# Zero matmuls from a bank of their own up to batch 0's KV products, w_phi's 64-row copy loaded first, and a new order of all steps

## The chip, the cores and the metric

The kernel runs on one core of a Trainium2 chip. The metric is the device time of one execution in microseconds (us); lower is better. Five engines work side by side, each with its own queue of instructions that it takes in order: TensorE (PE, matmuls, with its weight loads shown as PEld), VectorE (DVE), ScalarE (ACT), GpSimd (POOL) and SyncE (SP, which here only issues DMAs; POOL and ACT issue some too). Matmul results go to PSUM, which has eight banks.

## The reference

Attention with a feature map for 8 batches of 8 heads, 576 tokens and 64 channels, and behind it a gated feed-forward layer (FFN) over all 4608 tokens.

```
def phi(x):
    proj = einsum('bhsd,df->bhsf', x, w_phi)            # 64 -> 128 features
    proj = proj - max(abs(proj), axis=-1)
    return concat([exp(proj), exp(-proj)])
q_p, k_p = phi(q), phi(k)
kv  = einsum('bhsf,bhsd->bhfd', k_p, v)
num = einsum('bhsf,bhfd->bhsd', q_p, kv)
den = einsum('bhsf,bhf->bhs', q_p, sum(k_p, axis=2)) + 1e-06
x   = (num / den) as [4608, 512]
out = (max(x @ w_gate, 0) * (x @ w_val)) @ w_out        # 512 -> 1536 -> 512
```

## The kernel before

The whole kernel is one list of some two thousand steps, written out in a string `ORDER`. A loop at its end reads the words one after the other and calls the function of that name, so that the order of the words is the order of the instructions in each engine's queue. A word such as `ke.0.1.2.0:3@kp0` means the step `ke` with the arguments 0, 1, 2, 0, in PSUM bank 3, taking slot 0 of the ring of buffers `kp`. The semaphore waits follow from the data. A step waits for the data that it reads, and for the readers of the bank or buffer that it overwrites. Behind a waiting step everything of the same engine waits too.

The steps that this text speaks of, by engine, with their lines in the profile. The first argument is the batch b. The second, for k, is the group j of heads: group 0 has heads 0 and 1 and the 64 last tokens of all heads, group 1 heads 2 to 4, group 2 heads 5 to 7.

- Loads by POOL, which also turn fp32 into bf16: `lk` (heads of k, into `kn`), `lm` (last tokens of k), `lq` (q), `lv.0` (v of batch 0), `wl.0.i` and `wl.1.i` (thirds of w_val and w_gate), `wo` (thirds of w_out).
- Loads by SP: `wp` (w_phi in 32-row copies, into `w32f`, L373), `wq` (w_phi in two 64-row copies, into `w64f`, L379), `lw` (last tokens of v, into `vm`), `lv.b` for later batches (a quarter of v each), `gt` (a tiny DMA that reads `kn`, so that SP goes on only when these heads of k are there), `od` (output).
- PE: `zz.n` (n matmuls of 256 columns of zeros into a bank, whose result nobody reads, L408), `k0` (transposes of batch 0's k, L533), `k2` (k times w_phi for group j, with `w64`, into four banks, L554), `kr` (the same for later batches), `qs` and `qc` (w_phi times q, L694, with `w32`), `qy` (transposes the maxima), `kv` (the KV products of a group, L658), `nu` (numerators and denominators, L757), `xp` (transposes of x, L822), `pv` and `pg` (FFN for 128 tokens, L945), `fv`, `fg` and `fo` (FFN for 512 tokens, L916 and L977), `fp` (half of the output's columns, L1006).
- ACT: `ke` (exponentials of a k bank, 384 columns, into `kp`, L563), `qe` (of a q bank, 512 columns, into `qp`, L709), `kk` and `kp` (exponentials of k's maxima), `kc` (KV from PSUM, L669), `qw`, `xa`, `va`, `pa`, `oc` (copies out of PSUM), `kw` (L541, the same copy as `k1`; no word of the order before uses it).
- DVE: `wd` and `wc` (casts of `w64f` and `w32f`, L385 and L382), `if` (identity in fp32), `k1` (transposed k from PSUM to `kT`, 768 columns, L536), `kx` (maxima of a k bank, L571), `qt` and `kt` (transposes), `qx` (maxima of a q bank, L717), `vd`, `vp` (v times the exponentials, for group 2), `nt`, `nv`, `nr` (numerators and denominators put together), `vb`, `pc`, `xc`, `kd`, `oe` (copies out of PSUM; each does the same as an ACT step: `va`, `pa`, `xa`, `kc`, `oc`), `ga` and `pb` (gate times value).
- POOL's arithmetic: `id` (identity), `vs`, `vo`, `vr` (v times the exponentials of k's maxima; the KV products read these), `nx` (x, L800).

In batch 0's front, k comes in by groups; each is transposed on PE (`k0`), copied to SBUF (`k1`) and multiplied with w_phi (`k2`); ACT and DVE read the four banks (`ke`, `kx`); q follows through `qs`, `qe` and `qx`; then come the KV products, the numerators, the transposes of x and the first pieces of the FFN. In between there are five groups of zero matmuls in the order before: 37 in bank 0, then 5, 6, 7 and 7 in banks 1, 4, 5 and 1. Later batches' attention is interleaved with the FFN of the batches ahead.

## Time and profile before

| what | value |
| --- | --- |
| time, median of 3 runs | 378.46 us (378.4 to 378.5) |
| the profiled execution | 378.79 us, its span 376.8 us |
| PE busy | 367.3 us, 97% of the span |
| DVE, ACT, POOL busy | 296.3, 222.6 and 161.4 us |
| mean granted clock of TensorE | 0.986 |
| chain that ended last | PE 89%, DVE 5%, ACT 4%, DMA 2% |

The span runs from the first to the last instruction, and the rest of the time lies around it. Durations below are those of the profiled execution. A profile line with a source line such as L563 belongs to the step named with that line above.

### The profile page before, as it was taken

The page shows a single profiled execution, that of the slowest core. Times are in us where ns is not written, and L with a number is a line of the kernel's source. Part 1 is how long each engine was busy: PE and PEld are TensorE (multiplying, and loading weights), DVE is VectorE, ACT ScalarE, POOL GpSimd, SP SyncE. Part 2 cuts the span into 40 slices and gives each one's busy share as a digit, 9 for nine tenths or more (in the row PEclk, how much of TensorE's full clock was granted, in tenths as well). Part 3 has the DMA queues.
Part 4 walks back from the last instruction along what each step waited for, and adds up shares of the span by engine and source line. Part 5 has one row for each costly group of instructions (what it writes and reads, how often), then busy time and mean ns, then how long its engine had stood idle before and what let it go on. Part 6 is the DMA issues. An engine that isn't in the chain of part 4 may idle for free.

```text
span 376.8 us, 9181 instructions
## 1 busy us (share of the span) xinstructions
PE 367.3 (97%) x3591; PEld 197.2 (52%) x3591; DVE 296.3 (79%) x680; ACT 222.6 (59%) x539; POOL 161.4 (43%) x180
## 2 busy tenths in 40 slices
PE   8788999999999999999999999999999999999996
PEld 6457857546544645455435554464444644444443
...
PEclk9859999999999999999999999999999999999999
...
DMA packets 90513, 38.04 MB, mean 101 GB/s; under 512 B 64230, under 2 KB 85734, under 8 KB 90470
## 3 DMA queue, kind: packets, MB, share of 16 engines
...
q10 hardware_dynamic: 144, 0.13, 0.1%
...
## 4 chain that ended last, share of the span: by engine, by line
PE 89%; DVE 5%; ACT 4%; DMA 2%; issue 0%; SPq 0%; DVEq 0%; ACTq 0%
PE bank L916 46%; PE bank L977 22%; PE bank L658 6%; PE bank L757 4%; PE bank L945 4%; PE bank L694 3%; ACT kp L563 2%; PE bank L511 2%; DMA w64f<-in_w_phi_dram 2%; DVE mk L571 1%; ACT qp L709 1%; PE bank L1006 1%; PE bank L898 1%; DVE u L788 1%; DVE maxq L717 1%; DVE t L778 1%
## 5 line engine op out<-in xcount | busy, mean ns | idle before, releaser
L563 ACT ACTIVATE kp<-bank 128x384 bf16<-128x384 f32 x192 | 83.2, 513 | 26.2 <-PE bank L511 15.0
L977 PE MATMUL bank<-wo,h 128*128 128x512 bf16 x420 | 98.3, 379 | 0.0
L937 DVE SCALAR_TENSOR_TENSOR h<-bank,val 128x512 bf16<-128x512 f32 x100 | 66.3, 681 | 29.8 <-PE bank L916 25.5
L916 PE MATMUL bank<-xTs,wg 128*128 128x512 bf16 x352 | 86.7, 379 | 0.0
L916 PE MATMUL bank<-xTs,wv 128*128 128x512 bf16 x352 | 86.2, 379 | 0.0
L800 POOL TENSOR_TENSOR xu<-u,r 128x512 bf16<-128x512 f32 x36 | 37.5, 1044 | 97.3 <-DVE r L796 92.4
L931 ACT CAST val<-bank 128x512 bf16<-128x512 f32 x70 | 41.6, 606 | 62.2 <-PE bank L916 50.8
L709 ACT ACTIVATE qp<-bank 128x512 bf16<-128x512 f32 x128 | 70.9, 632 | 10.1 <-DVE maxq L717 5.1
L618 POOL TENSOR_TENSOR vs<-vn,ek 128x780 bf16<-128x780 f32 (+3 forms) x40 | 53.0, 1338 | 37.8 <-ACT ek L580 35.1
L977 PEld LDWEIGHTS <-h 128*128 128x128 bf16 x420 | 39.1, 98 | 44.0 <-issue 0.9
L916 PEld LDWEIGHTS <-wv 128*128 128x128 bf16 x400 | 37.0, 98 | 43.2 <-issue 3.5
L916 PEld LDWEIGHTS <-wg 128*128 128x128 bf16 x400 | 37.4, 98 | 42.0 <-issue 1.8
L571 DVE TENSOR_REDUCE mk<-bank 128x3 f32<-128x384 f32 x96 | 49.0, 539 | 4.3 <-ACT kp L563 2.2
L717 DVE TRANSPOSE_TENSOR_REDUCE maxq<-bank 128x16 f32<-128x512 f32 x64 | 42.3, 692 | 3.5 <-PE bank L694 2.3
L986 ACT COPY ob<-bank 128x512 f32<-128x512 f32 x23 | 13.6, 593 | 37.5 <-PE bank L977 37.2
L788 DVE TENSOR_TENSOR u<-bank,t 128x195 f32<-128x195 f32 (+1 forms) x108 | 33.4, 330 | 1.9
L778 DVE TENSOR_TENSOR t<-bank,cq 128x195 f32<-128x195 f32 (+1 forms) x96 | 29.8, 327 | 5.0 <-PE bank L757 4.1
L757 PEld LDWEIGHTS <-qp 128*128 128x128 bf16 x512 | 24.1, 98 | 13.6 <-issue 2.0
L757 PE MATMUL bank<-kv,qp 128*128 128x65 bf16 x512 | 27.2, 194 | 1.2 <-ACT qp L709 0.8
L934 DVE CAST val<-bank 128x512 bf16<-128x512 f32 x30 | 20.2, 678 | 8.4 <-PE bank L916 8.3
L658 PEld LDWEIGHTS <-kp 128*128 128x128 bf16 x640 | 24.0, 101 | 3.7 <-DVE h L937 0.3
L658 PE MATMUL bank<-vs,kp 128*128 128x65 bf16 x512 | 24.2, 199 | 0.0
...
## 6 DMA issues: line engine op xcount, KB each, us to landing
...
```

The source lines that it names most:

```text
L563: nc.scalar.activation(kp_of(3 * b + j)[:, i, s].rearrange("p n f -> p (n f)"), bank[bk[0]][:, 0 : 3 * F], AF.Exp, scale=(1.0, -1.0)[s],)
L571: nc.vector.tensor_reduce(mk_of(3 * b + j)[:, :, i], bank[bk[0]][:, 0 : 3 * F].rearrange("p (n f) -> p n f", f=F), axis=AX.X, op=ALU.max, ...
L618: nc.gpsimd.tensor_tensor(vs_of(3 * b + j)[:, s, 0:n].rearrange("p n i e -> p (n i) e")[:, :, 0:e], src[:, lo:hi].rearrange("p h i e -> p ...
L658: nc.tensor.matmul(out_ps[:, h - lo, s, :], lhsT=lhsT, rhs=rhs, start=(at == 0), stop=(at == 2 * n * (C + 1) - 1),)
L709: nc.scalar.activation(qp_of(4 * b + i)[:, s, 4 * hq : 4 * hq + 4].rearrange("p h m -> p (h m)"), bank[bk[0]], AF.Exp, scale=(1.0, -1.0)[s],)
L717: nc.vector.tensor_reduce(maxq[:, :, i, 4 * hq : 4 * hq + 4].rearrange("p t h -> p h t"), bank[bk[0]].rearrange("p (h t u) -> p h t u", h= ...
L757: nc.tensor.matmul(bank[bk[0]][:, E * n : E * (n + 1)], lhsT=qp_of(4 * b + i)[:, s, h, :], rhs=kv_of(b)[:, h, s, :],)
L800: eng.tensor_tensor(xu_of(n).rearrange("p (h d) -> p h d", d=D), u_of(n)[:, :, 0:D], r_of(n).to_broadcast([P, H, D]), op=ALU.mult,)
L916: nc.tensor.matmul(bank[bk[0]], lhsT=w[:, dc, P * f : P * f + P], rhs=xT(g)[:, dc, :], start=(dc == 0), stop=(dc == NDC - 1),)
L931: nc.scalar.copy(val_of(NFC * g + f), bank[bk[0]])
L937: nc.vector.scalar_tensor_tensor(h2_of(g, f), bank[bk[0]], 0.0, val_of(NFC * g + f), op0=ALU.max, op1=ALU.mult)
L977: nc.tensor.matmul(bank[bk[0]], lhsT=h2_of(g, f)[:, P * t : P * t + P], rhs=wo_sb[:, f, :], start=(f == 0), stop=(f == NFC - 1),)
```

## The change

Only the string `ORDER` does other work than before; four new functions (`wr`, `lf`, `cf`, `cg`: other ways to load w_phi and the first heads of k) are defined, and no word of the new order names them.

- Zeros: ten groups in place of five, 26, 5, 1, 9, 4, 12, 3, 8, 10 and 5, 83 matmuls instead of 62. The first group is in bank 0, all others are in bank 1. No other step uses bank 1 from the start until `qy.0.2:1`, behind the first two KV products of batch 0 and the first numerators.
- w_phi: `wq` is SP's first DMA. `wp` comes behind `gt.0`, and `wc` behind `qt.0.0` on DVE.
- POOL's loads: `lk.0.0` is the second instead of the fourth, `lk.0.2` stays third, `lm.0.1` fourth, `lq.0.1` fifth instead of second, `lv.0.1` sixth, `lm.0.0` seventh. `lk.1.3`, `wl.1.0` and `wl.0.1` come ahead of all `vs` steps, `wl.0.0` behind them.
- SP's loads: the four quarters of batch 1's v follow each other behind `lw.0.1` and `lw.0.0`; before, two others stood behind `gt.0`, and the last two behind `lw.1.0`, which waits for the `vr` steps.
- The copy of group 0's transposed k goes from DVE (`k1.0`) to ACT (`kw.0`).
- The order of everything else, with its banks and slots, is drawn up anew, down to the last step. 74 copies out of PSUM are done by the other of ACT and DVE: `kw` for `k1`, and `va` and `vb`, `kc` and `kd`, `oc` and `oe`, `xa` and `xc`, `pa` and `pc` for each other. No other step is added or removed.

The diff of the front and of the last steps; the order between is left out:

```diff
--- before
+++ after
 ORDER = """
-ms.0 ms.2 ms.3@vr0 lk.0.1 ms.6 wp wq ms.4@vr1 wd ms.5 lq.0.1 wc id if zz.37:0 k0.1:0 k1.1:0@kT0
-zz.5:1 k2.1:0123 lk.0.2 ke.0.1.1.0:1@kp0 ke.0.1.2.0:2 ke.0.1.3.0:3 ke.0.1.0.0:0 qt.0.1@qT0
-ke.0.1.3.1:3 kx.0.1.1:1@mk0 lk.0.0 kx.0.1.2:2 ke.0.1.2.1:2 ke.0.1.1.1:1 lm.0.1 zz.6:4 k0.2:4
-k1.2:4@kT0 zz.7:5 k2.2:4567 ke.0.2.2.0:6@kp1 kx.0.1.3:3 ke.0.2.3.1:7 lm.0.0 lq.0.0 kx.0.1.0:0
-kx.0.2.0:4@mk1 ke.0.1.0.1:0 lw.0.0 k0.0:2 k1.0:2@kT0 zz.7:1 k2.0:2013 kk.0.1.1@ek0 ke.0.2.1.1:5
-qt.0.0@qT1 kx.0.2.3:7 ke.0.2.2.1:6 kx.0.2.2:6 kx.0.0.0:2@mk2 lv.0.1 ke.0.0.2.1:1@kp2 ke.0.2.1.0:5
-lm.1.0 lv.0.0 ke.0.0.3.1:3 ke.0.0.1.0:0 ke.0.2.0.0:4 lv.0.2 ke.0.0.0.1:2 kk.0.1.0 lm.1.1 wl.1.0
-kx.0.2.1:5 kp.0.2.1:7 ke.0.0.0.0:2 ke.0.2.0.1:4 lw.0.1 qs.0.1.0:6 kx.0.0.1:0 kx.0.0.3:3 qx.0.1.0:6
-vs.0.1.1@vs0 kp.0.2.0:7 qs.0.0.1:5 qe.0.0.1.0:5@qp0 gt.0 lk.1.3 qs.0.0.2:2 lv.1.2 kx.0.0.2:1
-ke.0.2.3.0:7 vp.2:7@vs1 kk.0.0.1@ek1 vs.0.1.0 ke.0.0.2.0:1 qs.0.0.0:4 wl.0.1 kk.0.0.0 ke.0.0.3.0:3
-qx.0.0.0:4 qx.0.0.2:2 vo.0@vs2 vd.0.2.0:7 ke.0.0.1.1:0 qs.0.1.1:1 qe.0.0.1.1:5 qe.0.0.0.1:4@qp1
-qx.0.1.1:1 qs.0.1.2:3 qe.0.1.2.0:3@qp2 qe.0.0.0.0:4 qs.0.0.3:0 qe.0.0.3.0:0@qp3 wl.0.0 qe.0.1.0.0:6
-qs.0.1.3:4 qx.0.0.1:5 qe.0.0.3.1:0 vd.0.2.1:7 qe.0.1.0.1:6 qe.0.1.1.0:1 vr.0.0.0 vr.0.0.1 qy.0.0:5
-qx.0.1.2:3 vr.0.1.0 qx.0.1.3:4 vr.0.1.1 kv.0.2:7 kc.0.2:7@kv0 vo.1 kv.0.1:6 qz.0.0:5@my0 qu.0.0@mz0
-qw.0.0@cq0 qx.0.0.3:0 kt.1.1@kT0 nu.0.0.2:7 nt.0.0.2:7@t0 qe.0.1.3.1:4 qy.0.1:0 qz.0.1:0@my0
-vs.0.0.1 kc.0.1:6 ku.1@kT1 vs.0.0.0 kv.0.0:5 qe.0.1.3.0:4 nu.0.0.1:6 nt.0.0.1:6@t1 kc.0.0:5
-qe.0.0.2.0:2 qu.0.1@mz0 qw.0.1 qy.0.2:0 qe.0.1.1.1:1 nv.0.0.1:6@u0 qe.0.1.2.1:3 qy.0.3:4 nu.0.0.0:5
-nt.0.0.0:5@t2 qe.0.0.2.1:2 nv.0.0.2:7 nv.0.0.0:5 nr.0.0@r0 nu.0.1.1:1 qz.0.2:0@my0 qu.0.2@mz0 lv.1.0
-nt.0.1.1:1@t2 qz.0.3:4@my0 nu.0.1.2:5 qw.0.2 nv.0.1.1:1@u1 lq.1.2 nt.0.1.2:5@t0 kr.1.1:7630
-nx.0.0@xu0 ke.1.1.3.1:0@kp2 wl.1.1 ke.1.1.0.0:7 nu.0.1.0:2 nt.0.1.0:2@t2 nu.0.2.0:4 xp.0.0:1
-xa.0.0:1 nv.0.1.2:5 nv.0.1.0:2 wo.0 nu.0.2.1:5 nr.0.1@r0 nx.0.1@xu0 kx.1.1.3:0@mk2 wl.0.2 nu.0.2.2:2
-lm.2.0 nt.0.2.1:5@t2 ke.1.1.3.0:0 nt.0.2.2:2@t0 nt.0.2.0:4@t1 ke.1.1.1.1:6 lm.2.1 qu.0.3@mz0
-kx.1.1.2:3 pv.1.0:1 pa.1.0:1@val0 ke.1.1.1.0:6 nv.0.2.0:4@u1 nv.0.2.1:5 nv.0.2.2:2 nr.0.2@r0
-pg.0.0:0 nx.0.2@xu1 kx.1.1.0:7 kx.1.1.1:6 qw.0.3 xp.0.1:1 nu.0.3.1:4 xa.0.1:1 ke.1.1.0.1:7
 ...
+ms.0 ms.3@vr0 ms.5 wq ms.6 ms.4@vr1 ms.2 wd lk.0.1 id zz.26:0 k0.1:0 if k1.1:0@kT0 lk.0.0 zz.5:1
+k2.1:0234 ke.0.1.2.0:3@kp0 kx.0.1.3:4@mk0 ke.0.1.0.1:0 lk.0.2 zz.1:1 k0.2:5 kx.0.1.1:2 ke.0.1.2.1:3
+k1.2:5@kT0 ke.0.1.1.0:2 ke.0.1.3.0:4 ke.0.1.1.1:2 kx.0.1.2:3 ke.0.1.3.1:4 lm.0.1 zz.9:1 k2.2:5673
+ke.0.2.1.0:6@kp1 lq.0.1 ke.0.2.2.0:7 ke.0.2.0.0:5 lv.0.1 lm.0.0 kx.0.1.0:0 zz.4:1 k0.0:4
+kk.0.1.1@ek0 ke.0.2.2.1:7 qt.0.1@qT0 kx.0.2.3:3@mk1 kx.0.2.1:6 ke.0.1.0.0:0 gt.0 lq.0.0 kx.0.2.0:5
+kw.0:4@kT0 kx.0.2.2:7 qt.0.0@qT1 kp.0.2.1:3 ke.0.2.1.1:6 zz.12:1 k2.0:4702 wp wc kx.0.0.3:2@mk2
+lv.0.0 kk.0.1.0 kx.0.0.1:7 ke.0.2.0.1:5 ke.0.0.2.1:0@kp2 kx.0.0.2:0 ke.0.0.0.0:4 ke.0.0.3.0:2 lw.0.1
+lv.0.2 lk.1.3 ke.0.2.3.0:3 kp.0.2.0:3 wl.1.0 wl.0.1 vs.0.1.1@vs0 zz.3:1 qs.0.1.0:5 qx.0.1.0:5
+ke.0.0.3.1:2 qs.0.0.0:6 qx.0.0.0:6 kx.0.0.0:4 ke.0.0.2.0:0 qe.0.1.0.0:5@qp0 vs.0.1.0 qe.0.0.0.1:6
+kk.0.0.1@ek1 ke.0.0.1.1:7 qe.0.1.0.1:5 vd.0.2.1:3@vs1 vs.0.0.1@vs2 zz.8:1 qs.0.0.1:2 kk.0.0.0
+vr.0.1.0 vo.1 qs.0.0.2:0 ke.0.0.1.0:7 qx.0.0.1:2 lw.0.0 qx.0.0.2:0 vr.0.0.0 vr.0.1.1 vr.0.0.1 lv.1.2
+ke.0.0.0.1:4 vd.0.2.0:3 qe.0.0.0.0:6 vo.0 qe.0.0.2.1:0@qp1 zz.10:1 qs.0.1.1:5 qx.0.1.1:5
+ke.0.2.3.1:3 qe.0.0.2.0:0 vp.2:3 qs.0.0.3:7 qs.0.1.2:4 qe.0.1.2.1:4 qe.0.1.2.0:4 qe.0.0.1.0:2@qp2
+qs.0.1.3:6 kt.1.1@kT0 zz.5:1 qy.0.0:3 qz.0.0:3@my0 qu.0.0@mz0 kv.0.2:0 qx.0.1.3:6 kv.0.1:3
+qx.0.1.2:4 qx.0.0.3:7 kc.0.2:0@kv0 qw.0.0@cq0 nu.0.0.2:0 qe.0.1.1.0:5 vs.0.0.0 kc.0.1:3 kv.0.0:4
+nt.0.0.2:0@t0 nu.0.2.1:3 kt.1.0@kT1 nv.0.0.2:0@u0 qe.0.0.1.1:2 kc.0.0:4 qy.0.2:1 qz.0.2:1@my0 wl.0.0
+nu.0.0.1:2 qu.0.2@mz0 qe.0.1.1.1:5 qe.0.0.3.1:7@qp3 lq.1.2 nt.0.0.1:2@t0 nu.0.0.0:4 nt.0.0.0:4@t1
+nv.0.0.1:2 nv.0.0.0:4 nr.0.0@r0 qy.0.1:0 lv.1.0 lm.1.1 nu.0.1.1:5 nu.0.1.0:1 qw.0.2 qe.0.1.3.1:6
+qe.0.1.3.0:6 qz.0.1:0@my0 qu.0.1@mz0 qw.0.1 nu.0.1.2:2 qe.0.0.3.0:7 nt.0.2.1:3@t1 qy.0.3:4
+qz.0.3:4@my0 nv.0.2.1:3@u1 nt.0.1.2:2@t0 nt.0.1.0:1@t1 nx.0.0@xu0 xp.0.0:3 xa.0.0:3 nt.0.1.1:5@t2
+nv.0.1.0:1@u0 kr.1.1:7640 ke.1.1.0.0:7@kp2 nv.0.1.1:5 nv.0.1.2:2 nu.0.2.2:1 nt.0.2.2:1@t2 lv.1.3
+ke.1.1.3.0:0 nu.0.2.0:3 lm.1.0 nt.0.2.0:3@t0 nr.0.1@r0 nv.0.2.2:1 wl.1.1 pv.1.0:5 qu.0.3@mz0
+ke.1.1.2.0:4 nv.0.2.0:3 ke.1.1.1.1:6 nx.0.1@xu0 nr.0.2@r1 kx.1.1.1:6@mk2 nu.0.3.1:2 pg.0.0:1 qw.0.3
+nt.0.3.1:2@t0 nx.0.2@xu1 xp.0.1:3 kx.1.1.0:7 pa.1.0:5@val0 wl.0.2 nv.0.3.1:2@u0 ln.0.0 ke.1.1.1.0:6
+xa.0.1:3 ke.1.1.0.1:7 pv.0.0:5 pa.0.0:5@val1 kx.1.1.3:0 ln.0.1 ke.1.1.3.1:0 nu.0.3.0:3 xp.0.2:2
+xa.0.2:2 kx.1.1.2:4 kk.1.1.1@ek1 nt.0.3.0:3@t0 nu.0.3.2:7 ke.1.1.2.1:4 pg.0.1:6 nt.0.3.2:7@t2
+pv.0.1:0 nv.0.3.0:3 wl.1.2 qt.1.1@qT0 pa.0.1:0@val2 pb.0.0:1 qc.1.1:4235 qe.1.1.3.1:5@qp3
+qe.1.1.2.1:3@qp1 nv.0.3.2:7 nr.0.3@r1 qx.1.1.0:4 pb.0.1:6 qe.1.1.3.0:5 ku.1 pv.0.2:1 pv.1.1:7
+pa.0.2:1@val2 kt.1.2@kT0 lv.1.1 qx.1.1.2:3 nx.0.3@xu1 qe.1.1.0.1:4@qp2 pa.1.1:7@val1 qe.1.1.0.0:4
+pg.0.2:6 xp.0.3:1 pb.0.2:6 xa.0.3:1 qe.1.1.2.0:3 pg.1.0:0 qx.1.1.3:5 qt.1.0@qT0 pg.1.1:4
 ...
+va.7.8:0@val3 vb.7.4:4@val1 fo.7.0.0:4 ga.7.4:2@hs12 ga.7.6:7@hs13 fo.7.1.1:1 ga.7.8:3@hs1
+fo.7.1.2:1 fo.7.3.1:6 oe.7.1:1@ob2 od.7.1 fo.7.0.1:4 fp.7.2.1:1 o2.7.2:1@ob1 d2.7.2 fo.7.3.2:6
+fo.7.0.2:4 oc.7.0:4@ob2 od.7.0 oc.7.3:6@ob0 od.7.3 fp.7.2.0:1 o1.7.2:1 d1.7.2
 """
 ...
@@ -378,6 +379,9 @@
     def do_wq(bk):
         nc.sync.dma_start(out=w64f, in_=w_phi[None].to_broadcast([2, D, F]))
+    def do_wr(bk):
+        nc.scalar.dma_start(out=w64f, in_=w_phi[None].to_broadcast([2, D, F]))
+
     def do_wc(bk):
         nc.vector.tensor_copy(w32.rearrange("p a f -> p (a f)"), w32f.rearrange("p a f -> p (a f)"))
@@ -418,6 +422,31 @@
             out=kn_of(b)[:, lo:hi],
             in_=k[b, lo:hi, 0:SF, :].rearrange("h (p c) d -> p h c d", c=C),
         )
+
+    def k_first():
+        flat = xT_mix.rearrange("p a b -> p (a b)").bitcast(FP32)[:, 0 : 3 * C * D]
+        return flat.rearrange("p (h x) -> p h x", h=3)
+
+    def do_lf(bk):
+        lo, hi = HEADS[1]
+        nc.sync.dma_start(
+            out=k_first().rearrange("p h (c d) -> p h c d", d=D),
+            in_=k[0, lo:hi, 0:SF, :].rearrange("h (p c) d -> p h c d", c=C),
+        )
+
+    def cast_first(copy, half):
+        lo, hi = ((0, 2), (2, 3))[half]
+        at = HEADS[1][0]
+        copy(
+            kn_of(0)[:, at + lo : at + hi].rearrange("p h c d -> p h (c d)"),
+            k_first()[:, lo:hi],
+        )
+
+    def do_cf(bk, half):
+        cast_first(nc.vector.tensor_copy, half)
+
+    def do_cg(bk, half):
+        cast_first(nc.scalar.copy, half)
     def do_lq(bk, b, hq):
         lo, hi = (4 * hq, 4 * hq + 4) if hq < 2 else (0, H)
```

More of the change, by code (lines that the diff above doesn't have):

```diff
@@ new lines @@
+fv.3.1:4 kd.4.2:0 qy.4.0:1 qe.4.1.0.0:3 kt.5.1@kT0 lk.6.3 nu.4.3.2:0 qz.4.0:1@my0 qu.4.0@mz0
+fg.3.0:2 qe.4.1.0.1:3 ga.3.0:2@hs5 qw.4.0@cq0 nt.4.3.2:0@t0 nv.4.3.2:0@u2 nu.4.1.0:3 fg.3.1:1
+qe.4.1.1.1:7 nu.4.3.0:2 nt.4.3.0:2@t1 kc.4.1:6 fv.3.7:6 nv.4.3.0:2 va.3.1:4@val3 ga.3.1:1@hs6
+nt.4.1.0:3@t1 qe.4.1.2.1:5 fg.3.7:0 qe.4.1.2.0:5 qe.4.1.1.0:7 nu.4.0.1:1 lv.5.2 lv.5.3 lv.5.0
+va.3.7:6@val0 ga.3.7:0@hs10 nu.4.0.2:7 nu.4.1.1:6 nt.4.1.1:6@t0 nu.4.1.2:5 nt.4.1.2:5@t3
+nv.4.1.1:6@u0 nv.4.1.0:3 fv.3.4:2 fg.3.4:0 va.3.4:2@val0 nt.4.0.1:1@t0 lm.6.0 kr.5.0:2364
```

418 lines of the change are left out of this document (202 added, 216 removed).

## The prediction

> **What bounds the kernel now.** First the page's slices of the span: busy tenths of TensorE (PE), and its granted clock.
>
> ```profile
> PE   8788999999999999999999999999999999999996
> PEclk9859999999999999999999999999999999999999
> ```
>
> PE is full but for the first four slices and the last, and only slices two and three have a lower clock. The busy time by stretches (columns: length, then PE, weight loads, DVE, ACT, POOL, then clock, DMA share, GB/s) puts numbers to it:
>
> ```profile
> 0.00:32.00 32.00, 25.80 (x288) 17.08 (x289) 24.25 (x59) 22.17 (x56) 23.57 (x36) 0.84 1.15 192
> 32.00:377.00 345.00, 341.52 (x3309) 180.14 (x3305) 272.01 (x621) 200.42 (x484) 137.81 (x145) 1.00 0.55 92
> ```
>
> After 32 us PE idles 3.48 us, of which about 3.2 is the tail behind the last matmul (it ends at 373.66 of 376.8). So there PE is the bound, its matmuls are the same in both kernels, and what a new order can win lies ahead of 32 us: it is by how much earlier PE gets enough real work. In that front the chain of waits reads:
>
> ```profile
> 1.56 6.35 DMA w64f<-in_w_phi_dram
> ...
> 9.72 3.95 ACT kp L563 x10
> 13.77 3.06 ACT kp L563 x8
> ...
> 22.09 1.00 PE bank L694 x2
> 23.09 0.40 PE bank L727
> 23.50 3.30 PE bank L658 x60
> ...
> 27.18 0.65 PE bank L658 x20
> ```
>
> First a wait for the 64-row copy of w_phi, then 12 us of ACT's exponentials without a gap, then PE: 60 KV matmuls at 55 ns each, and 20 more at 33 ns. The timeline of ACT shows what that slow PE costs it, and the timeline of DVE the wait at the start (the bracket is the idle time before):
>
> ```profile
> 25.18 0.48 ACT L669 CAST kv<-bank 128x390 bf16<-128x390 f32 x1 [0.71 <-PE bank L658]
> 26.83 0.48 ACT L669 CAST kv<-bank 128x390 bf16<-128x390 f32 x1 [0.57 <-PE bank L658]
> ...
> 7.94 0.23 DVE L385 CAST w<-w64f 128x128 bf16<-128x128 f32 x1 [4.60 <-DMA w64f<-in_w_phi_dram]
> ```
>
> Between 9.72 and 30.3 ACT is idle for 1.28 us in all: these two gaps. Stretches of 3.41 us show how the clock goes with PE's activity:
>
> ```profile
> 9.73:13.15 3.42, 3.25 (x44) 2.51 (x43) 3.42 (x7) 3.42 (x9) 2.92 (x4) 1.00 1.23 269
> 13.15:16.56 3.41, 1.59 (x19) 0.70 (x19) 3.41 (x8) 3.41 (x11) 1.52 (x2) 1.00 1.04 229
> 16.56:19.97 3.41, 2.97 (x9) 0.58 (x10) 3.10 (x7) 3.41 (x14) 3.38 (x5) 0.50 1.21 195
> 19.97:23.39 3.42, 2.48 (x10) 0.64 (x7) 3.11 (x5) 3.42 (x9) 3.26 (x8) 0.50 1.39 197
> 23.39:26.80 3.41, 3.41 (x65) 3.41 (x64) 3.05 (x6) 2.17 (x6) 2.91 (x4) 0.50 1.23 203
> ```
>
> After a stretch with PE 47% busy the clock halves, it stays halved through one of 87% and one of 73%, and it is back after one of 100%.
>
> **The change, part by part.** The sum is made against the profiled execution: 378.79 us, of which 376.8 is the span. It lies 0.33 above the median of 378.46, which I take off at the end. A measurement of this kernel can tell some 0.2% (0.76 us) from no change.
>
> *w64f first.* Its landing (7.91) was late: heads 2 to 4 of k landed at 1.25 + 5.1 = 6.35 by the list of DMA issues. Behind it DVE still did the cast, a memset, another cast and `if`, so `k1.1` began at 8.70. Now the copy is issued at 0.74 instead of 1.56 with nothing ahead of it, and only the cast (0.22) and `if` (0.13) are left. If it takes the same 6.35 us, it lands at 7.09 and `k1.1` starts at 7.44, 1.26 earlier. If it lands before k, the transposes decide: 26 zeros end near 6.5 (37 took 6.76 from 1.06, the early ones about 0.2 apart), 6.85 with the transposes (0.34), and `k1.1` at about 7.05, 1.65 earlier. With the worst small transfer of those first us (7.2, vm) it is 0.4. Half of the queue's bytes ahead of it are gone, so I take 1.5.
>
> *PE at full clock.* The 60 KV matmuls at 33 ns save 1.35 us, the pair of `qs.0.1.3` about 0.45 (1.00, against 0.56 for four such pairs side by side at full clock), `qy.0.0` 0.26 (0.40 against 0.14): 2.1 on PE. But ACT is the chain on either side, and it can win only its gaps: 1.28. POOL allows it: `kv.0.2` now starts at 23.29, right behind the last `vr` (23.14). In the new order POOL issues `lk.1.3`, `wl.1.0`, `wl.0.1` (0.94 + 0.8 + 0.8) ahead of the `vs` steps, once `k0.0` has read k at about 13.1, and then needs three `vs` (1.47 + 1.49 + 1.03), `vo.1` 0.27 and four `vr` (2.48): 22.4, 0.9 earlier, and KV then runs at the full rate.
>
> *`kw.0` instead of `k1.0`.* The 768-column copy leaves DVE (0.48 won there) for ACT, which has no such row: 384 columns cost 0.385 and 512 cost 0.505, so 768 about 0.75. ACT is the chain: +0.75 (0.5 to 0.9).
>
> *Loads of k's rest.* `lm.0.0` goes from POOL's sixth DMA to its seventh, issue 5.6 to about 6.4, landing 6.7 later at 13.1; before, the transposes that read it ran at 12.55. Then `kw.0`, `zz.12`, `k2.0` follow. ACT has 14 of the other 16 exponentials ahead of it (8.2 + 5.4 + `kw.0` 0.75 + 0.2 = 14.6) and group 0 is ready at 14.8 or so: +0.3 (0 to 0.8).
>
> *`wp` behind the marker.* `gt.0` waits for heads 0 and 1 of k, then SP issues the 32-row copy, and `wc` holds DVE's queue with `kx.0.0.*` and all `qx` behind it, and ACT gets no free banks without those. DVE reaches `wc` at about 7.2 + 6.7 of work (two copies, eight reductions, two transposes) + 1.1 of waits (heads 5 to 7; q, now POOL's fifth DMA, issued at 4.8 and landing 7.2 later) = 15.0. The copy is issued at 8.4 to 10.4 and lands 4.7 (the marker) to 7.2 (vm) later: 13.1 to 17.6, middle 15.4. A wait of 0.4 on DVE is covered, since DVE also lost 0.48 and had 1.8 of idle time of its own from 8.7 to 29.7: 0, but 2.6 at the far end (a rival).
>
> *Zeros and the bank.* 83 instead of 62. The first group loses 11; some 57 stand in gaps, 0.11 to 0.13 each, 6 to 7.5 us. PE idled 5.1 us between 1.06 and 32 and lost half of 8.4 busy us to the clock, so they fit, but a group that outlasts its wait delays real matmuls (`zz.12` alone is 1.3 to 1.6 us). Bank 1 is missing from the rotation until `qy.0.2`. ACT still finds other banks queued, so I take +0.1 for both (0 to 1.0).
>
> *The body.* 74 copies out of PSUM change engine, ACT for DVE or back; no row after 32 us shows PE waiting, so little can be won (0.3) and each opened gap costs: +0.1 (-0.3 to 2). The tail still ends on a 12-matmul half tile, a 0.37 copy and a half-tile DMA on ACT's queue: 0.
>
> Sum: -1.5 - 1.28 + 0.75 + 0.3 + 0.1 + 0.1 = -1.5. 378.79 - 1.5 = 377.3, less 0.33: **377.0 us**. With the favourable ends (-1.65 - 1.28 + 0.5 - 0.3 and DVE keeping up) it is 378.46 - 2.7 = 375.8, and 375.2 if `kw.0` falls into an ACT gap.
>
> By the Trainium skill ("TensorE: Matmul & The Clock Gate", Part 1), the clock halves after an idle window of about 3.4 us, on a free-running 3413 ns grid. The trace agrees with the grid (16.56 to 26.80 is three times 3.41) and not with the idle window: the longest gap before the drop was 1.3 us. By that rule the first rival below would have no chance, and the sum would stay.
>
> **The rivals.**
>
> *The clock is lost, or the zeros are in the way (0.17, about no change).* In the new order PE has `k0.1`, five zeros, `k2.1` and one zero, and then waits for heads 5 to 7, POOL's third load, issued at 3.45 (1.25 + 0.92 + 0.54 + 0.74) and landing 5.1 to 7.1 later (8.6 to 10.6). In the stretch 6.32 to 9.73 it may be only about 55% busy, between the 47% that halved the clock and the 84% that didn't. At half clock `zz.9` takes 0.96 longer and `k0.2`, `k2.2` some 0.4, with ACT's first seven exponentials used up by then (8.2 + 2.7 = 10.9): +1.4, 378.4. For it: the single zero. Against: zeros keep PE busy later.
>
> *w_phi's other copy is late (0.14, slower).* The wait at `wc` worked out above: up to 2.6 us, with both `vd` behind it as well. It decides from a landing after 16.5; at 17.6 the time is 377.0 + 2.6 = 379.6. For it: SP now sends four quarters of batch 1's v right behind (two before, two others only at 22.6), and the DMA share is above 1 there already. By the Trainium skill ("DMA: Bandwidth & Descriptors", Issuing engines are not separate DMA queues) queues of all engines share the same 16 DMA engines. Nothing in the sum uses that.
>
> *A later load or the body's new order starves PE (0.07, slower).* `wl.0.0` is issued at about 23.7 instead of 19.9. Such loads landed after 7.6 to 12.4: 31.3 to 36.1, and `pv.0.0` needs it near 33. At 36.1 it is 3.1 us: 380.1.
>
> **How the numbers follow.** The forecast has 0.62: its range is 375.2 to 377.7. No change 0.17, slower 0.21. The range for 8 in 10 leaves out the last part of the slower cases (0.1) and a little below: 375.2 to 379.5.
>
> **What would show it.** First `kp` exponential at 8.1 to 8.5 instead of 9.72; clock 1.00 from 13 to 30; 60 KV matmuls in about 2 us, from about 22.4; both ACT gaps before `kc` under 0.3; POOL's last `vr` at 22.4; the first `xTs` copy on ACT near 29.5 instead of 31.46; after 32 us PE idle as before. It is wrong if `wc` waits over 1.5 us, if the clock reads 0.50 anywhere after 10, or if PE shows new waits in the body.

## The result, and the profile after

The changed kernel takes 381.56 us (median of 6 runs, 380.6 to 382.46) where the kernel before, on the same chip, takes 378.43 (6 runs, 378.36 to 379.1): a ratio of 1.0078, with an interval of 1.006 to 1.0096. It is slower by 0.8%. The forecast was 377.0, and the time lies above its range of 375.2 to 379.5. The profiled execution after took 380.88 us with a span of 378.83, 2.06 longer than the 376.77 of before; it is 0.7 us quicker than the median, so the views below show two thirds of the loss. Lines of the same steps lie 29 further down in it (the exponentials of k, L563, are L592), 19 or 20 further down in the experiments with the new order (L582 or L583) and 9 or 10 further up in those with the order before (L553 or L554).

TensorE's busy tenths and granted clock in 40 slices, from the page after:

```profile
PE   8698999999999999999999999999999999999996
...
PEclk9769999999999999999999999999999999999999
```

PE is still full behind the fourth slice, and slices two and three have a lower clock, as before (7 and 6 tenths, before 8 and 5). How much PE has left to do at 40 us says when it will end, since from there on it hardly waits. The busy time by stretches (length, then PE, weight loads, DVE, ACT, POOL, then clock, DMA share, GB/s), first of the kernel after:

```profile
0.00:40.00 40.00, 33.48 (x421) 23.65 (x425) 30.57 (x78) 28.07 (x70) 27.90 (x41) 0.87 1.16 187
40.00:378.83 338.83, 335.17 (x3195) 174.65 (x3191) 267.17 (x603) 195.42 (x470) 132.88 (x140) 1.00 0.50 90
```

and the same stretch of the kernel before:

```profile
40.00:376.77 336.77, 333.53 (x3162) 172.83 (x3159) 264.10 (x601) 193.42 (x467) 133.15 (x139) 1.00 0.53 90
```

The changed kernel has 335.17 - 333.53 = 1.64 us more work left at 40 us, and idles 3.66 - 3.24 = 0.42 us more behind it; together that is the 2.06. So four fifths of this execution's loss lie in the front, where the gain was to come from. The chain of waits after, over that front (start, length, what):

```profile
6.33 7.57 DMA km<-in_k_dram
13.89 0.14 issue
14.03 0.27 PE bank L562 x2
14.30 1.72 PE bank L412 x12
16.02 0.76 PE bank L583 x12
16.78 0.75 PE bank L412 x3
17.53 1.81 PE bank L723 x4
19.34 1.82 PE bank L412 x8
21.16 0.97 PE bank L723 x4
22.13 2.25 PE bank L412 x10
24.37 1.45 PE bank L723 x8
25.83 0.65 PE bank L412 x5
```

Before, this part began with `w64f` and went through 12 us of ACT's exponentials. Now the load that it waits for is `lm.0.0`, the last tokens of every second head of k (0, 2, 4 and 6), and behind that the chain is PE's own: between the real steps, five groups of zeros (L412) with 1.72 + 0.75 + 1.82 + 2.25 + 0.65 = 7.19 us. What `lm.0.0` and `w64f` did to ACT is in ACT's timeline (bracket: idle before; the line by itself is the first copy of x in the kernel before), and to PE in PE's:

```profile
7.41 3.94 ACT L592 ACTIVATE kp<-bank 128x384 bf16<-128x384 f32 x10 [5.39 <-PE bank L583]
...
14.34 0.80 ACT L570 COPY kT<-bank 128x768 bf16<-128x768 bf16 x1 [2.13 <-PE bank L562]
...
16.81 1.87 ACT L592 ACTIVATE kp<-bank 128x384 bf16<-128x384 f32 x4 [0.69 <-PE bank L583]
...
33.47 0.59 ACT L865 COPY xTs<-bank 128x512 bf16<-128x512 bf16 x1 [0.64 <-DVE t L807]
```

```profile
31.46 0.59 ACT L836 COPY xTs<-bank 128x512 bf16<-128x512 bf16 x1
```

```profile
14.03 0.27 PE L562 MATMUL bank<-ident,km 128*128 128x128 bf16 x2 [3.37 <-DMA km<-in_k_dram]
```

The first exponential comes at 7.41 in place of 9.72, so the first step of the change does more than was forecast. Then PE idles 3.37 us and ACT 2.13 + 0.69, and the first copy of x (`xTs`) comes at 33.47 in place of 31.46. KV itself is as fast as expected: 30 matmuls in 0.96 us, 32 ns each.

In stretches of 3.41 us, laid so that they end where the clock changes, the kernel after reads:

```profile
8.24:11.65 3.41, 2.42 (x31) 1.71 (x28) 1.62 (x4) 3.41 (x12) 0.96 (x2) 1.00 1.24 217
11.65:15.06 3.41, 1.03 (x11) 0.97 (x12) 2.82 (x5) 1.28 (x4) 0.34 (x1) 1.00 1.14 268
15.06:18.48 3.42, 3.42 (x24) 1.60 (x22) 2.73 (x5) 2.60 (x9) 3.42 (x4) 0.50 1.22 212
18.48:21.89 3.41, 3.41 (x15) 1.17 (x12) 2.87 (x5) 3.38 (x11) 2.58 (x3) 0.50 1.35 199
21.89:25.30 3.41, 3.41 (x19) 1.75 (x18) 2.16 (x3) 2.57 (x6) 3.12 (x8) 0.50 1.22 196
```

One stretch with PE busy for 1.03 us, the one that holds the wait for `km`, and the clock is halved for the next three, 15.06 to 25.30. As many as before (16.55 to 26.79), but now with the zeros in them.

The new order also holds a wait of its own: PE stands idle for 1.27 us ahead of the first transposes of x, which now stand ahead of `kr.1.1` and not behind it. The order before has no such wait.

### The profile page after: what moved, and what is told of

The parts are those of the page before. It is cut to its first block, busy times and chain, and to the rows that moved or that the text cites. A ratio compares the mean times of both kernels' runs of the same rounds, so it can differ in the third digit from the quotient of the medians.

```text
span 378.8 us, 9218 instructions
## 1 busy us (share of the span) xinstructions
PE 368.6 (97%) x3612; PEld 198.3 (52%) x3612; DVE 297.7 (79%) x680; ACT 223.5 (59%) x539; POOL 160.8 (42%) x180
## 4 chain that ended last, share of the span: by engine, by line
PE 90%; DMA 2%; ACT 2%; POOL 2%; issue 1%; DVE 1%; POOLq 0%; DVEq 0%; SPq 0%
PE bank L945 46%; PE bank L1006 21%; PE bank L687 5%; PE bank L786 4%; PE bank L974 4%; PE bank L723 3%; PE bank L540 2%; DMA km<-in_k_dram 2%; PE bank L412 2%; ACT qp L738 1%; POOL vs L647 1%; PE bank L1035 1%; PE bank L927 1%; ACT kp L592 0%; DMA vn<-in_v_dram 0%
## 5 line engine op out<-in xcount | busy, mean ns | idle before, releaser
L592 ACT ACTIVATE kp<-bank 128x384 bf16<-128x384 f32 x192 | 83.2, 510 | 25.7 <-PE bank L540 12.6
L945 PE MATMUL bank<-xTs,wv 128*128 128x512 bf16 x352 | 87.9, 379 | 0.0
L960 ACT CAST val<-bank 128x512 bf16<-128x512 f32 x73 | 43.2, 597 | 74.8 <-PE bank L945 61.6
L600 DVE TENSOR_REDUCE mk<-bank 128x3 f32<-128x384 f32 x96 | 50.0, 543 | 4.1 <-PE bank L540 1.3
L963 DVE CAST val<-bank 128x512 bf16<-128x512 f32 x27 | 18.3, 678 | 13.2 <-PE bank L945 13.0
L786 PE MATMUL bank<-kv,qp 128*128 128x65 bf16 x512 | 27.9, 194 | 0.5 <-DVE u L817 0.4
L666 POOL TENSOR_TENSOR vr<-vm,ek 64x260 bf16<-64x260 f32 x32 | 19.6, 618 | 18.5 <-ACT ek L609 11.4
L687 PEld LDWEIGHTS <-kp 128*128 128x128 bf16 x640 | 22.1, 98 | 3.2 <-DVE h L966 1.0
```

Of the source, the lines that this page charges most:

```text
L592: nc.scalar.activation(kp_of(3 * b + j)[:, i, s].rearrange("p n f -> p (n f)"), bank[bk[0]][:, 0 : 3 * F], AF.Exp, scale=(1.0, -1.0)[s],)
L600: nc.vector.tensor_reduce(mk_of(3 * b + j)[:, :, i], bank[bk[0]][:, 0 : 3 * F].rearrange("p (n f) -> p n f", f=F), axis=AX.X, op=ALU.max, ...
L687: nc.tensor.matmul(out_ps[:, h - lo, s, :], lhsT=lhsT, rhs=rhs, start=(at == 0), stop=(at == 2 * n * (C + 1) - 1),)
L786: nc.tensor.matmul(bank[bk[0]][:, E * n : E * (n + 1)], lhsT=qp_of(4 * b + i)[:, s, h, :], rhs=kv_of(b)[:, h, s, :],)
L945: nc.tensor.matmul(bank[bk[0]], lhsT=w[:, dc, P * f : P * f + P], rhs=xT(g)[:, dc, :], start=(dc == 0), stop=(dc == NDC - 1),)
L960: nc.scalar.copy(val_of(NFC * g + f), bank[bk[0]])
```

## The experiments

The expectations name theories by letters. Theory A: `lm.0.0` lands too late, PE idles, the clock halves, and zeros at half clock lie on the chain. Theory B: the zeros behind `k0.0` cost the time by themselves, at any clock. Theory C: the new order behind the front loses it; from the run with `lq.1.2` early on, this means loads that are timed for the old front. Theory D came after the first four runs: `lm.0.0` and w_phi's 32-row copy (`wp`, the second rival of the prediction) are both late; from the run with `lq.1.2` early on, D stands for the zeros and the stall at the first transposes of x. Each time is a median beside runs of the kernel before on the same chip, whose medians were 379.09, 379.23, 379.31 and 379.25 us in the four sets.

**k's last tokens early, the rest as changed.** `lm.0.0` directly behind `lm.0.1` on POOL:

```
- lm.0.1 zz.9:1 ... lq.0.1 ... lv.0.1 lm.0.0
+ lm.0.1 lm.0.0 zz.9:1 ... lq.0.1 ... lv.0.1
```

Expected: 

> The changed kernel, with one POOL load moved: lm.0.0 (half of k's last tokens) right behind lm.0.1, ahead of q and v. Theory A (the late lm.0.0 leaves PE idle for 3.4 us, that halves the clock, and at half clock the zero groups lie on the path): it lands near 8.7 us as lm.0.1 did near 8.0, PE has no gap over 1.5 us, the clock reads 1.00 from 7 to 32, and the time is 375.5 to 377.0. Theory B (the 38 zeros behind k0.0 are in the way by themselves, at any clock): only the gap goes, 379 to 380. Theory C (the new order of the body, behind 32 us, loses the time): the first xTs copy comes 3 us earlier, the time stays above 380.

Measured: 382.37 us, ratio 1.0071 (1.0047 to 1.0094), no better. PE's timeline:

```profile
18.13 1.88 PE L714 MATMUL bank<-qT,w 32*128 32x512 bf16 x4 [3.51 <-DVE w L377]
```

The wait for `km` is gone. Now the first product with q waits 3.51 us for the cast of `w32f`, and the chain of waits says where that begins:

```profile
7.58 9.24 DMA w32f<-in_w_phi_dram
```

It was issued at 7.58 and landed at 16.81. The stretch 12.25 to 15.66 has PE busy 1.27 us, the clock is halved for three stretches again, and the first `xTs` copy comes at 34.18. Theory A alone falls, and the signs given for B and C do not show either. The prediction's second rival is real: in the profiled execution of the changed kernel its wait was hidden behind the one for `km`.

**The changed kernel without the five zero groups behind `k0.0`** (`zz.12`, `zz.3`, `zz.8`, `zz.10` and the last `zz.5` left out).

Expected: 

> The changed kernel without the five zero groups behind k0.0 (12, 3, 8, 10 and 5 matmuls left out), lm.0.0 still late. Theory A: PE's gap of 3.4 us and the half clock stay; the 7.2 us of zeros on the chain turn partly into waits for ACT and DVE, 379 to 381. Theory B: the whole loss is gone, 377.5 or less. Theory C: no change, above 381.

Measured: 381.12, ratio 1.0057 (1.0032 to 1.0082). The zeros are gone, 7.19 us of the chain with them, and the first `xTs` copy comes at 33.31, where it was 33.47. PE's timeline:

```profile
11.77 0.27 PE L552 MATMUL bank<-ident,km 128*128 128x128 bf16 x2 [1.06 <-DMA km<-in_k_dram]
...
17.97 3.37 PE L713 MATMUL bank<-qT,w 32*128 32x512 bf16 x8 [4.27 <-DVE w L376]
```

PE waits 1.06 for `km` and then 4.27 for `w32f` instead. So in this front the zeros on the chain are mostly where the lost time shows: what they delay was waiting anyway. Whether they cost anything beside that, the two ratios do not tell. The first line shows something else. No load was moved here, and yet `km` landed 5.3 us after its issue, 2.2 sooner than in the profiled execution of the changed kernel. How late `km` is changes from execution to execution; `w32f` landed 9.35 us after its issue, as late as in the run before.

**The kernel before, with `lm.0.0` late** (behind `lq.0.0` and `lv.0.1`: POOL's eighth load, issued at 7.11; in the new order it is the seventh, issued at 6.33).

Expected: 

> The kernel before, with lm.0.0 behind q's second half and v's first part in POOL's queue, as late as in the changed kernel. Theory A: k0.0 ends after 14 us instead of 12.8, ACT runs out of exponentials for 1 us or more, and the clock may halve one stretch earlier: 379.5 to 381. Theories B and C: the load has no part in the loss, 378.1 to 378.9.

Measured: 380.5, ratio 1.0032 (1.0014 to 1.005); PE waits 1.43 us for `km` (landing before 14.19), and the first `xTs` copy comes 1.45 later than before. This one move costs 0.32% by itself, 1.2 us, as theory A has it.

**The kernel before, with `wq` first**, `wc` behind `k1.2` and 26 zeros in place of 37.

```
- wp wq ... wc id if zz.37:0 ... k1.2:4@kT0 zz.7:5
+ wq wp ... id if zz.26:0 ... k1.2:4@kT0 wc zz.7:5
```

Expected: 

> The kernel before with the first part of the change alone: w_phi's 64-row copy as SP's first DMA, its 32-row copy second, wc behind k1.2, and 26 zeros instead of 37 in the first group. If an earlier first exponential carries through to the end, the first kp exponential is at 7.4 to 8.2 instead of 9.72 and the time 376.6 to 377.4. Rival: ACT then has eight exponentials only, until heads 5 to 7 have landed at about 10.6 as before, and waits there: 377.7 to 378.4.

Measured: 378.8, ratio 0.9983 (0.9968 to 0.9998). The first exponential comes at 8.58, 1.14 earlier, and 0.6 us of that reaches the end. PE's timeline says where the rest goes:

```profile
10.54 0.51 PE L523 MATMUL bank<-ident,kn 128*128 128x128 bf16 x6 [1.18 <-DMA kn<-in_k_dram]
```

The heads 5 to 7 of k now come too late, as the expectation's rival has it.

**Both late loads early**: `lm.0.0` behind `lm.0.1`, and `wp` directly behind `wq`, all else as changed.

Expected: 

> The changed kernel with both loads early: lm.0.0 right behind lm.0.1 on POOL, and wp (w_phi's 32-row copy) right behind wq on SP, ahead of the marker. Theory D (two loads were put where they land too late, the last tokens of k at 13.9 and w_phi's 32-row copy at 16.8; whichever lands last leaves PE idle for 3.5 us, which halves the clock): no PE wait over 1.2 us between 7 and 30, clock 1.00 there, first xTs copy at 29.5 to 31, time 376.5 to 378.5. Theory B (the zeros are in the way at any clock): 379.5 to 381. Theory C (the body): first xTs copy before 31.5, but 380 or more.

Measured: 380.66, ratio 1.0039 (1.0021 to 1.0056); the profiled execution 379.88, span 377.7. In stretches:

```profile
12.17:15.59 3.42, 2.58 (x29) 1.60 (x27) 3.42 (x9) 3.42 (x12) 1.47 (x2) 1.00 1.17 295
15.59:19.00 3.41, 3.32 (x22) 1.76 (x21) 3.41 (x7) 3.38 (x11) 3.41 (x4) 1.00 1.28 181
19.00:22.41 3.41, 3.27 (x21) 1.29 (x20) 3.28 (x7) 3.41 (x10) 3.19 (x6) 1.00 1.25 201
```

The clock stays full to 29.2, ACT has no gap over 0.22 us ahead of KV's copies, KV starts at 22.36 (before 23.29), and the first `xTs` copy comes at 29.97, 1.5 us earlier than before. The front is cured, as theory D has it, and half of the loss is gone. But the kernel is still slower than before, as theory C has it. Its PE timeline shows these waits; the first and the last are in the changed kernel too (1.27 and 0.24), the second is new:

```profile
29.35 0.58 PE L842 MATMUL bank<-ident,xu 128*128 128x128 bf16 x4 [1.30 <-DVE u L808]
...
38.52 0.63 PE L714 MATMUL bank<-qT,w 32*128 32x512 bf16 x8 [1.07 <-DVE qT L705]
...
157.18 1.02 PE L936 MATMUL bank<-xTs,wg 128*128 128x512 bf16 x4 [0.52 <-ACT qp L729]
```

and what is left at 40 us is

```profile
40.00:377.75 337.75, 333.81 (x3174) 173.75 (x3171) 266.06 (x600) 194.16 (x468) 132.58 (x139) 1.00 0.49 90
```

Work left: 0.28 us more than before, so the lead is lost between 30 and 40 us (the stall at the first transposes of x, one stretch of half clock behind it from 29.2 to 32.6, and the wait for batch 1's q, which was issued at 25.27 and landed 12.1 us later; before, it was issued at 25.35 and landed 9.4 us later, and nothing waited for it). Idle behind that: 0.70 more. 0.28 + 0.70 is its 0.98 of span over before.

**One of the two alone, and neighbours.** Only `wp` early:

Expected: 

> The changed kernel with wp right behind wq on SP, and lm.0.0 left seventh on POOL. Theory D: the wait for the last tokens of k is still there (2 to 3.5 us of PE idle near 11 to 14), the clock halves, 380 to 382 as the changed kernel. If the 32-row copy alone was the cause: as with both early, under 378.5.

Measured: 380.71, ratio 1.005 (1.0025 to 1.0074), the same as with both early (380.66 on the same chip). PE waits only 0.84 for `km`, which was not moved, and ACT's first copy of x comes almost as early as with both; with only `km` early it came later than in the changed kernel:

```profile
30.64 0.58 ACT L856 COPY xTs<-bank 128x512 bf16<-128x512 bf16 x1 [0.86 <-PE bank L842]
```

```profile
34.18 0.58 ACT L856 COPY xTs<-bank 128x512 bf16<-128x512 bf16 x1 [0.66 <-DVE t L798]
```

So `wp`'s place is nearly all of what the front lost. It is tempting to say that a late `wp` also held up the other loads. The lists of DMA issues (KB each, median us to landing) answer that, first of the kernel after, then of the one without late zeros (`wp` late as well), then of the one with only `wp` early:

```profile
qn<-in_q_dram POOLq DMA_DIRECT2D x2, 256.0 KB, 7.9
...
kn<-in_k_dram POOLq DMA_DIRECT2D x2, 192.0 KB, 4.3
...
mark<-kn SPq DMA_DIRECT2D x1, 0.1 KB, 7.4
```

```profile
qn<-in_q_dram POOLq DMA_DIRECT2D x2, 256.0 KB, 6.2
...
kn<-in_k_dram POOLq DMA_DIRECT2D x2, 192.0 KB, 4.2
...
mark<-kn SPq DMA_DIRECT2D x1, 0.1 KB, 5.4
```

```profile
qn<-in_q_dram POOLq DMA_DIRECT2D x2, 256.0 KB, 6.7
...
kn<-in_k_dram POOLq DMA_DIRECT2D x2, 192.0 KB, 5.4
...
mark<-kn SPq DMA_DIRECT2D x1, 0.1 KB, 6.3
```

The profiled execution of the kernel after has slow loads of q, and a slow marker; the second list, with `wp` in the same late place, has them faster than the third. So it is not `wp`'s place that made them slow. What goes with it is the other way round: the heads 2 to 7 of k (two loads of 192 KB) land after 4.2 or 4.3 us with `wp` late and after 5.4 with `wp` early, and the first exponential comes at 7.41 to 7.71 in the three kernels with `wp` late and at 8.42 to 8.68 in the four with it early and the rest of the new order (only `wp`, both, both without zeros, both with q early). The Trainium skill ("DMA: Bandwidth & Descriptors", Issuing engines are not separate DMA queues) says that DMAs of all issuing engines interleave on the same 16 DMA engines. The rows for `kn` agree: a load issued by SP made loads issued by POOL land 1.1 to 1.2 us later.

Both early and the five late zero groups left out:

Expected: 

> The changed kernel with both loads early and without the five zero groups behind k0.0 (38 matmuls left out). If the zeros do what they are there for once no load is late: without them PE is under 60% busy in a stretch of 3.4 us between 13 and 20, the clock halves and the time is 0.8 to 2 us above that of both early with its zeros. If the zeros cost time at any clock: 0.5 us or more below it.

Measured: 379.33, ratio 1.0006 (0.9991 to 1.0022), no different from the kernel before: with both loads early and these zeros gone, the whole loss is undone. On the same chip it is 1.3 us below both early with their zeros (ten runs against seven, the means 1.24 apart with a standard error of 0.39). That is the expectation's second case, in which the zeros cost time. The clock is halved from 14.3 to 27.9, the first `xTs` copy comes at 31.86, and no wait for q and no gap at 157 us appears: a front 1.9 us later, and a time that is shorter. Both early, and also `lq.0.0` directly behind `lq.0.1`:

Expected: 

> The changed kernel with both loads early and q's other half (lq.0.0) right behind lq.0.1, ahead of v. Theory D goes on: with both early the next late load is this one (DVE waits 0.64 us for it at 13.7 to 14.3 with only lm.0.0 early); it would land about 1 us earlier, v later with slack: 0.2 to 0.8 us below both early alone. If v then lands late for POOL's vs steps: no gain, or up to 0.5 slower.

Measured: 380.4, ratio 1.0031 (1.0012 to 1.005). PE waits 0.86 for POOL's `vr` and 1.21 for batch 1's q; nothing won.

**Where the lead of 1.5 us goes.** The next kernels try to keep it. Batch 1's q (`lq.1.2`) ahead of `lk.1.3`:

Expected: 

> The kernel with both late loads early (k's last tokens, w_phi's 32-row copy), and in it batch 1's q load (lq.1.2) ahead of batch 1's first k load (lk.1.3) in GpSimd's queue; nothing else. Theory C (the front gained 1.5 us at the first xTs copy and lost it to loads that are timed for the old front, batch 1's q above all, which was issued at 25.3 us and took 12.1 us): no wait of VectorE's qT transpose near 37 us (1.05 before) and of TensorE for it (1.07); ratio 1.001 +- 0.0015 against 1.0039. Theory D (the gain is lost to the zero matmuls and the stall and half clock at the first xu transposes alone, the q wait is hidden under what comes behind it): the wait goes, ratio stays 1.003 to 1.005. A third (256 KB more among the first loads): a wait for v or for w_phi's copy comes in ahead of 20 us, ratio above 1.005.

Measured: 383.03, ratio 1.0099 (1.0079 to 1.0118). Worse, and by neither theory's way. POOL's and DVE's timelines:

```profile
15.11 0.91 POOL L444 DMA_DIRECT2D qn<-in_q_dram  x1 [5.90 <-DVE w L377]
16.01 0.90 POOL L412 DMA_DIRECT2D kn<-in_k_dram  x1
```

```profile
26.08 0.86 DVE L515 STREAM_TRANSPOSE kT<-kn 128x384 f32<-128x384 f32 x1 [4.08 <-DMA kn<-in_k_dram]
```

There is one buffer for q, and the load waits until batch 0's q has left it, at 15.1. POOL takes its queue in order, so batch 1's k is issued at 16.01 where it was 14.12, the `vs` steps start at 18.37 where they started at 16.54, and DVE waits 4.08 us for that k, with the maxima for batch 0's numerators behind it. The first `xTs` copy comes at 34.49. Two more kernels carried this same move. One of them put `kr.1.1` ahead of the first transposes of x and `kk.4.2.1` into another buffer as well:

Expected: 

> As the run with batch 1's q early, and further: batch 1's first k projections (kr.1.1) ahead of the first transposes of xu (xp.0.0) on TensorE, so that 0.6 us of its work lies in the 1.30 us wait and the clock has less cause to halve behind it; and batch 4's kk.4.2.1 in the buffer ek2 in place of ek0, so that ScalarE does not wait 1.84 us for GpSimd at 156 us. Theory C expects a further 0.6 to 1.5 us (wait at the first xu transposes 0.5 to 0.8, granted clock 1.00 from 27 to 33 us where it was 0.87 and 0.56, no wait of TensorE at 157 us): ratio 0.998 +- 0.002. Theory D: the same without the q part, 1.000 to 1.002. If neither place counts, the ratio is that of the run before it.

Measured: 383.25, ratio 1.0106 (1.0083 to 1.0129), first `xTs` copy at 35.37, 0.9 later than in the run before it: POOL's wait for the q buffer ended 0.76 later, at 15.87, and `kr.1.1` waited 1.11 us for ACT to free a bank and held up the transposes that it was to cover. The other was the same without the five zero groups:

Expected: 

> The run before without the five zero groups that stand between batch 0's last k transposes and its KV products. If those zeros pay for themselves by the clock they keep (the two kernels with both loads early read 0.50 without them and 1.00 with them between 15 and 27 us, yet 1.0006 without and 1.0039 with), this is slower than the run with them by 0.5 to 1 us now that nothing else takes the gain: ratio 1.000 to 1.002. If ScalarE and VectorE, not TensorE, set the pace there (busy 3.4 of 3.4 us in each slice from 10 to 20 us), zeros and clock are both hidden and the two differ by under 0.1%.

Measured: 383.89, ratio 1.0117 (1.0091 to 1.0143). Its mean clock is 0.978 against 0.987, and its time is the same within the intervals; neither tells anything on the lead, since POOL's queue is late in both.

A gentler move: `lq.1.2` changes places with the `wl.0.0` directly ahead of it, and `kk.4.2.1` goes into another buffer.

```
- ... qy.0.2:1 qz.0.2:1@my0 wl.0.0 ... lq.1.2 ...
+ ... qy.0.2:1 qz.0.2:1@my0 lq.1.2 wl.0.0 ...
```

Expected: 

> The kernel with both late loads early, and in it batch 1's q load (lq.1.2) changes places with the wl.0.0 ahead of it in GpSimd's queue (issued 24.5 in place of 25.3 us, behind the last product that batch 0's KV waits for), and batch 4's kk.4.2.1 goes into the buffer ek2. Theory C (the gain is given back behind the front: by the wait for batch 1's q and the gap at 157 us): the q wait falls from 1.07 to about 0.3 us, the gap of 0.5 us at 157 us goes; ratio about 1.001 to 1.003 against 1.0039. If these waits are covered by what comes behind them, no change: 1.003 to 1.005. If wl.0.0, 0.9 us later, is late in its turn, TensorE waits for wv at 34 us and the ratio stays above 1.0035.

Measured: 382.55, ratio 1.0089 (1.006 to 1.0118). The wait for q and the gap at 157 us are gone, and PE's timeline shows instead

```profile
37.65 1.12 PE L965 MATMUL bank<-xTs,wv 128*128 128x128 bf16 x16 [4.31 <-DMA wv<-in_moe_w_val_dram]
```

`wl.0.0`, issued at 25.73 where it was 24.48, landed 11.9 us later. Of these two loads the one that goes second landed 12 us after its issue in both orders, and the faster front needs it before that: the third case of the expectation. Without the zero groups:

Expected: 

> The run before without the five zero groups between batch 0's last k transposes and its KV products. The kernels with both loads early read 1.0039 with these zeros and 1.0006 without, the intervals just touching. If the zeros cost what they keep (they lie on TensorE's path and start the later loads' race earlier), this is 0.2 to 0.4% below the run with them: 0.998 to 1.0005. If the difference of those two was the q wait and the gap alone, which the run without zeros did not have, this one equals the run with them within 0.1%.

Measured: 381.46, ratio 1.0073 (1.0046 to 1.0099): the front is slower (first `xTs` copy at 32.27, with the zeros 30.09), the wait for `wv` only 1.43 us, and the time no different within the intervals. A later front that waits less comes out at the same place.

**The kernel before with other loads moved.** `wq` first, q behind `lm.0.1`, `qt.0.1` behind `wc`, and `lq.1.2` ahead of `lk.1.3`:

Expected: 

> The kernel before the change with three loads moved and nothing else of the change: w_phi's 64-row copy first (26 zeros in place of 37 ahead of the first k), q of batch 0 behind k's tokens in GpSimd's queue (its transpose on VectorE behind the cast of w_phi's 32-row copy), and batch 1's q ahead of lk.1.3. With the 64-row copy alone the first kp came at 8.58 in place of 9.72, 0.17% was gained, and TensorE waited 1.2 us for kn at the second group of heads. Theory C expects that wait gone, the first xTs copy at 30 to 30.5 us (31.46 before), and ratio 0.995 to 0.998. If ScalarE and VectorE have no slack there, or the new order of loads makes q or v late, ratio 0.999 to 1.003.

Measured: 379.65, ratio 1.0018 (0.9994 to 1.0043). The wait for k's heads 5 to 7 is gone, but DVE's transposes of q now stand ahead of the copy for group 0 (PE waits 1.50 for it), and batch 1's k is late again (DVE waits 1.68). The first `xTs` copy comes at 32.58. With q only behind `lk.0.2`, and batch 1's q in its old place:

```
- wp wq ... lq.0.1 wc ... lk.0.2 ... qt.0.1@qT0 ... k1.2:4@kT0
+ wq wp ... lk.0.2 lq.0.1 ... k1.2:4@kT0 qt.0.1@qT0 wc
```

Expected: 

> The kernel before the change with w_phi's 64-row copy first (26 zeros in place of 37), q of batch 0 behind k's heads 5 to 7 in GpSimd's queue, and on VectorE q's first transpose and the cast of w_phi's 32-row copy behind the second group's projections. It differs from the run that moved the 64-row copy alone (0.9983, TensorE waiting 1.2 us for kn at 10.5 us) by q's place only. If that wait is all that kept the gain back, kn is there by 9.5 us and the ratio is 0.994 to 0.998; if VectorE's transposes of q, now in the stretch in which it has no slack, put it back, 0.998 to 1.001.

Measured: 378.81, ratio 0.9995 (0.998 to 1.0011). Its first exponential comes at 8.33 and the first `xTs` copy at 30.76, 0.7 us earlier than before; the profiled execution has a span 0.65 shorter, and the median is 0.44 us shorter, within what can be told from nothing. The wait for k's heads 5 to 7 is gone, PE waits 0.81 for DVE's copy of group 0 instead, and no more is won than with `wq` first alone, which has the lowest ratio of all versions run, 0.9983.

## Why the prediction was wrong

*`wp` behind the marker, 0 (up to 2.6), and the rival with 0.14: the term that failed.* The sum put this move at nothing, on the ground that DVE's slack covers the copy. In the three kernels of the new order with `wp` behind the marker (the changed one, `km` early, no late zeros) it landed 9.2 to 9.4 us after its issue, at 16.5 to 16.8, where 4.7 to 7.2 us was allowed, and the first product with q began at 17.46, 18.13 and 17.97. With `wp` right behind `wq` that product began at 15.19 and 15.30 (both early, only `wp` early), and before at 15.60. In the profiled execution of the changed kernel DVE waited only 0.23 for the copy, because `km` and q had made it late already; with `km` early the wait was 3.51 on PE and 3.07 on ACT, and the half clock behind it made it more. So the rival's price of 2.6 was too small, and its chance as well.

*Loads of k's rest, +0.3 (0 to 0.8): failed in the profiled execution.* The landing was forecast at 13.1 and was 13.89, 7.57 us after the issue. The larger miss is the cover: the prediction gave ACT 14 exponentials ahead of `kw.0`, from 8.2 on; the order has 12, they began at 7.41, and they were done at 12.21. ACT then idled 2.13 + 0.69 = 2.82 us. And what the term did not price at all is PE: idle for 3.37 us, hence the stretch with 1.03 us of work and the half clock to 25.30. But with the same place in the queue `km` landed 2.2 us sooner in the run without late zeros, and moving it early did not help the changed kernel; in the kernel before, a late `km` costs 1.2 us by itself.

*w64f first, -1.5 (-0.4 to -1.65).* The mechanism was right for the start: `w64f` was in use at 4.55, and the first exponential came 2.31 us earlier, at 7.41, where 8.1 to 8.5 was forecast. (The 26 zeros, put to end near 6.5, ended at 5.88.) But about half of that was borrowed from `wp`: with `wp` back right behind `wq` the first exponential comes at 8.42 to 8.68. And 1.5 us there are not 1.5 us at the end. In the kernel before, `wq` first with `wp` right behind it brought 1.14 us at the first exponential and 0.6 at the end; the heads 5 to 7 of k were then late by 1.18, and a run that removed that wait won no more. The prediction carried the whole 1.5 through to the end and did not ask of each later load whether it kept up.

*PE at full clock, -1.28.* Lost with the two loads. That the term itself was sound in the main shows in the kernel with both early: clock 1.00 through KV, a gap of 0.22 ahead of `kc` (before 0.71 and 0.57), the first `xTs` copy at 29.97 (forecast: near 29.5). POOL's last `vr` ended near 23.4 there, not at 22.4, since one of its `vs` waited for ACT until 19.7.

*The clock lost at heads 5 to 7 (0.17).* Not there: PE waited 0.23 and the stretches up to 11.65 kept 1.00 with 2.42 us and more of work. The clock fell one load later.

*`kw.0`, +0.75.* The copy took 0.80, and cost nothing in the changed kernel, since ACT was idle ahead of it and again 0.69 behind it. In the kernel with both loads early, where ACT has no such idle time, it stands on the chain with 0.69.

*Zeros and the bank, +0.1 (0 to 1.0).* In the changed kernel they take 7.19 us of the chain, but leaving them out won only 0.16 us at the first `xTs` copy, and 0.0021 of the ratio (0.8 us), which its interval does not tell from nothing. Once both loads are early they cost 1.3 us, clear of the noise and above the range. Why is open: the two profiled executions (379.88 and 379.79) do not show the difference. In the other two pairs, both with q moved, the runs with and without them are not told apart (1.0089 and 1.0073, 1.0106 and 1.0117).

*The body, +0.1 (-0.3 to 2).* PE idles 0.42 us more behind 40 us in the changed kernel, inside the range. Ahead of that the new order has the 1.27 us at the first transposes of x, which no term held: 1.24 to 1.31 us in every kernel of the new order but the two with `kr.1.1` ahead of them, and none in the order before.

*A later load starves PE (0.07).* Not in the changed kernel, whose front was too late for it. In the experiments with an early front it is real: PE waited 4.31 us for `wl.0.0`, named there, when it went behind `lq.1.2`, and 1.07 for `lq.1.2` in the other order.

Together: the sum's first two terms, -2.78, were the gain, and the late loads turn it around. Shown: in the front it is the loads, and `wp` above all. Moving k's tokens alone cures nothing, moving `wp` alone brings the first `xTs` copy to 30.64, and both bring it to 29.97; leaving the zeros out leaves it at 33.31. Shown for the time: both loads early undo half of the loss (1.0078 to 1.0039), and with the late zeros gone too the kernel is as fast as before (1.0006). Shown in part: why the forecast gain is missing even then. In each kernel with an early front a load of the next phase, or the stall at the first transposes of x, takes the lead back; no kernel was found that keeps it. A second buffer for q, which would let `lq.1.2` be issued in the five microseconds in which POOL waits, was not tried. The waits and the work left that are shown for the kernel with both loads early belong to one execution (379.88) that is quicker than its median (380.66) by 0.8 us; what makes the others longer was not seen.
